# Input transform of a convolution, Fourier and MLP kernel: eight input pieces in four buffers instead of four pieces in two

## The chip, the cores and the metric

The kernel runs on one core of a Trainium2 chip. The time is device microseconds (us) of one execution; a kernel's time is the median of its runs. Before the change the median of three runs is 1305.61 us (1303.28, 1305.61 and 1310.38).

## The reference, cut to what matters

The input x has 8 batches of 4224 tokens with 192 features. Eight heads of 24 features each get a causal convolution over seven tokens, with softmaxed weights. On its result follow a Fourier transform over tokens and features, a layer norm and an MLP of 768 hidden units:

```python
    x_unf = x_pad[:, idx, :].reshape(B, S, K, H, group)
    out = np.einsum('hk,bskhg->bshg', w, x_unf)      # convolution
...
    X = np.fft.fft(x, axis=1)
    X = np.fft.fft(X, axis=2)
    mixed = np.real(X).astype(np.float32)
    u = x + mixed
    mu = np.mean(u, axis=-1, keepdims=True)
    var = np.mean((u - mu) ** 2, axis=-1, keepdims=True)
    un = (u - mu) / np.sqrt(var + 1e-06)
    ch = np.maximum(un @ w_ch1, 0.0) @ w_ch2
    return (u + ch).astype(np.float32)
```

## The kernel before

The work is done batch by batch, and each batch passes through stages:

- **Convolution** (`conv_unit`, matmul at L389). Six chunks a batch, each in three parts; an input tile `xt` is multiplied with a band matrix, copied out of the accumulators into `xa` (by ScalarE, L397) and stored from there to a scratch tensor `sc` in device memory. `squares` (L345) sums squares of the input, from which `scales` makes the batch's scale. Batch 7 does its last head in another way, on VectorE (`conv_segments`), and stores that with L423.
- **Loading the transform's input** (`load_x`, L458). The scratch is read back with another layout: 128 partitions by 33 blocks of 192 values. Before the change the 33 blocks are cut into four pieces of 9, 8, 8 and 8 (`PIECES`), each read by four transfers of 32 partitions. The pieces lie in tiles `xs`, for which there are two buffers. So piece 2 can only be loaded when the splits of piece 0 have been done.
- **Split** (`split_x`). ScalarE writes the high half of an input as float16 to `XH` (L474), VectorE the remainder to `XL` (L475). Each piece is split in two halves of 4 or 5 blocks. `XH` and `XL` exist once; they hold a whole batch.
- **Stage A** (`stage_a`, matmul at L492, then L500 on ScalarE and L501 on VectorE): sixteen units a batch, the first part of the Fourier transform over tokens. It needs all 33 blocks, so all splits. **Stage B** (`stage_b`, L518, L526, L527): eight units a batch.
- **Prep** (`prep`): the transform over features (L608), the addition to the convolution's rows `u` (L625; the rows were fetched from the scratch by L553 and, indirectly, by GpSimd at L557), the norm (L632, L633, and GpSimd at L643 to L665), and a transposing DMA `kt<-hl` (L675) issued by SyncE.
- **MLP** (`mlp_hidden`, matmul L704 into `ph`, ScalarE's `hh` at L708, VectorE's `hlo` at L709; `mlp_out`, matmuls L723, L726, L729 into `po`, VectorE L735), then the store of `u` by SyncE (L743). `ph` has two buffers, and one becomes free when `hlo` has read it.

The main loop has 72 steps: nine steps `it` = 0 to 8 for each of eight batches, the ninth (`it` = 8) a short one with a quarter of the tokens. In step n stand the hidden layer of step n and the output layer of step n-1; between their units are spread the other batches' earlier stages, by tables that tell at which step, counted relative to the first step of their own batch, a stage is done (`conv_at`, `load_at`, `split_at`, `a_at`, `b_at`; `load_1`, `split_1`, `a_1` for batch 1). So `load_at = {-10: [0], -9: [1, 2], -8: [3]}` puts the load of piece 0 ten steps ahead of its own batch. Batch 0 is worked through ahead of the loop, without anything to lie beside.

From this the program's order on each engine is made by a scheduler when the kernel is built; it may draw an instruction forward when its operands and buffers are there, or let it stand later. What it makes is a fixed list for each engine. An engine works its list in order, and so does SyncE (SP): a DMA that waits for a buffer holds up every DMA that stands behind it on SP.

## Time and profile before

| | |
|---|---|
| median of three runs | 1305.61 us |
| the profiled execution's own time | 1310.74 us |
| its span, from first to last instruction | 1308.4 us |
| TensorE (PE) busy | 1191.7 us, 91% |
| VectorE (DVE) busy | 828.9 us, 63% |
| GpSimd (POOL) busy | 794.4 us, 61% |
| ScalarE (ACT) busy | 585.2 us, 45% |
| mean granted TensorE clock | 0.963 |
| DMA | 130 GB/s mean, up to 277 GB/s in a fortieth of the span |

The rows of the profile name an engine, a line of the kernel, and the tiles as out<-in. "Idle before" is the engine's idle time ahead of an instruction, and the arrow names what ended it. Lines in the waits view read: who waited, for whom, us in total, times, longest. The windows view gives for a stretch of time its length, then the busy time of each engine with the number of instructions, the granted clock (1.00 is full, 0.50 half), the DMA engines' busy share and their rate. SPq and ACTq are DMA issues on those engines.

### The profile page before, as it was taken

The page shows a single profiled execution, that of the slowest core. Times are in us where ns is not written, and L with a number is a line of the kernel's source. Part 1 is how long each engine was busy: PE and PEld are TensorE (multiplying, and loading weights), DVE is VectorE, ACT ScalarE, POOL GpSimd, SP SyncE. Part 2 cuts the span into 40 slices and gives each one's busy share as a digit, 9 for nine tenths or more (in the row PEclk, how much of TensorE's full clock was granted, in tenths as well). Part 3 has the DMA queues.
Part 4 walks back from the last instruction along what each step waited for, and adds up shares of the span by engine and source line. Part 5 has one row for each costly group of instructions (what it writes and reads, how often), then busy time and mean ns, then how long its engine had stood idle before and what let it go on. Part 6 is the DMA issues. An engine that isn't in the chain of part 4 may idle for free.

```text
span 1308.4 us, 30213 instructions
## 1 busy us (share of the span) xinstructions
PE 1191.7 (91%) x12224; PEld 938.2 (72%) x12224; DVE 828.9 (63%) x1883; ACT 585.2 (45%) x962; POOL 794.4 (61%) x1116
## 2 busy tenths in 40 slices
PE   4168889997999989999899989999889998999998
PEld 4156768785877768787677858778677876778767
DVE  7746586467555776467755676556865678666543
ACT  4632375336543464435544355444644445333222
POOL 0236666577645785468664777547955589657850
PEclk9578999998999989999899999999899999999999
DMA  8924966357546465446644664563664444323231
GB/s 277 263 69 107 206 182 160 109 129 159 127 122 135 122 156 153 127 104 176 133 132 107 140 177 105 145 129 100 167 150 117 121 101 91 84 65 87 56 75 40
DMA packets 238363, 170.29 MB, mean 130 GB/s; under 512 B 119688, under 2 KB 222032, under 8 KB 238224
## 3 DMA queue, kind: packets, MB, share of 16 engines
q1 hardware_dynamic: 182096, 121.22, 38.5%
q10 hardware_dynamic: 49600, 33.77, 9.3%
q0 software_dynamic: 6528, 13.38, 3.9%
q8 instruction: 95, 1.56, 0.5%
q14 instruction: 44, 0.36, 0.1%
HBM read 83.82 MB, written 58.55 MB: 109 GB/s over the span
## 4 chain that ended last, share of the span: by engine, by line
PE 74%; DMA 9%; DVE 8%; ACT 3%; issue 2%; another core or an unknown queue 1%; ACTq 1%; POOL 1%; SPq 1%; DVEq 0%; POOLq 0%
PE ph L704 28%; PE po L723 8%; PE po L729 8%; PE po L726 8%; DMA xs<-sc 6%; PE pa L492 6%; PE pc L389 5%; PE pb L518 5%; PE pq L608 5%; DVE XL L475 3%; DVE u L625 2%; ACT XH L474 2%; DMA sc<-xa 1%; DVE hlo L709 1%
## 5 line engine op out<-in xcount | busy, mean ns | idle before, releaser
L704 PE MATMUL ph<-kt,W 128*128 128x512 f16 (+1 forms) x2160 | 504.9, 367 | 22.3 <-DVE hlo L709 17.1
L709 DVE SCALAR_TENSOR_TENSOR hlo<-ph,hh 128x512 f16<-128x512 f32 (+1 forms) x400 | 272.3, 681 | 295.6 <-ACT hh L708 274.1
L708 ACT ACTIVATE hh<-ph 128x512 f16<-128x512 f32 (+1 forms) x400 | 236.2, 592 | 453.0 <-PE ph L704 408.0
L723 PE MATMUL po<-W,hh 128*128 128x192 f16 x1584 | 387.8, 247 | 16.9 <-ACT hh L708 16.7
L729 PE MATMUL po<-W,hlo 128*128 128x192 f16 x1584 | 387.3, 247 | 1.5 <-DVE hlo L709 1.2
L726 PE MATMUL po<-W,hh 128*128 128x192 f16 x1584 | 387.4, 247 | 0.0
L704 PEld LDWEIGHTS <-W 128*128 128x128 f16 x2160 | 194.5, 99 | 169.9 <-issue 20.5
L652 POOL TENSOR_SCALAR un<-u,mv,y 128x192 f32<-128x192 f32 x264 | 279.0, 1063 | 7.9 <-POOL y L648 0.2
L557 POOL DMA_INDIRECT u<-sc,rows_sb x136 | 144.6, 1063 | 195.5 <-DMA xt<-in_xw_dram 56.4
L723 PEld LDWEIGHTS <-hh 128*128 128x128 f16 x1584 | 156.1, 99 | 40.2 <-ACT hh L708 18.5
L729 PEld LDWEIGHTS <-hlo 128*128 128x128 f16 x1584 | 155.7, 98 | 22.8 <-issue 1.8
L726 PEld LDWEIGHTS <-hh 128*128 128x128 f16 x1584 | 155.6, 98 | 16.6 <-issue 0.7
L389 PE MATMUL pc<-xt,band 128*120 128x144 f32 x756 | 116.2, 295 | 25.8 <-DMA band<-line_d 14.8
L492 PE MATMUL pa<-c_sb,XH 128*128 128x128 f16 x1024 | 105.0, 224 | 31.3 <-ACT XH L474 18.3
L389 PEld LDWEIGHTS pc<-xt,band 128*120 128x120 f32 x756 | 104.2, 188 | 35.2 <-issue 16.0
L475 DVE SCALAR_TENSOR_TENSOR XL<-xs,s_x,XH 128x768 f16<-128x768 f32 x64 | 102.8, 1620 | 41.2 <-ACT XH L474 41.1
L665 POOL TENSOR_TENSOR hl<-un,hl 128x512 f16<-128x512 f32 (+1 forms) x144 | 122.2, 870 | 2.8
L474 ACT ACTIVATE XH<-xs,s_x 128x768 f16<-128x768 f32 x64 | 105.4, 1689 | 26.6 <-DMA xs<-sc 26.6
L501 DVE SCALAR_TENSOR_TENSOR yl<-pa,yh 99x512 f16<-99x512 f32 x128 | 85.7, 684 | 46.0 <-ACT yh L500 35.8
L500 ACT ACTIVATE yh<-pa 99x512 f16<-99x512 f32 x128 | 75.5, 598 | 87.3 <-PE pa L492 63.6
L643 POOL TENSOR_SCALAR v<-mv 128x4 f32<-128x4 f32 (+1 forms) x72 | 20.7, 287 | 152.9 <-DVE mv L633 150.2
L492 PEld LDWEIGHTS <-XH 128*128 128x128 f16 x1024 | 83.2, 100 | 38.6 <-ACT XH L474 18.4
(120 smaller groups left out, 1496.2 us busy)
## 6 DMA issues: line engine op xcount, KB each, us to landing
out_dram<-u SPq DMA_DIRECT2D x64, 384.0 KB
xt<-in_xw_dram SPq DMA_DIRECT2D x42, 576.0 KB
sc<-xa ACTq DMA_DIRECT2D x42, 540.0 KB
xs<-sc SPq DMA_DIRECT2D x96, 192.0 KB
xs<-sc SPq DMA_DIRECT2D x32, 216.0 KB
u<-sc SPq DMA_DIRECT2D x72, 96.0 KB
sc<-xa ACTq DMA_DIRECT2D x7, 450.0 KB
xt<-in_xv_dram SPq DMA_DIRECT2D x6, 504.0 KB
```

Source lines behind the costliest of these rows:

```text
L389: nc.tensor.matmul(pc[:WR, h - h0], band[:, h, :WR], xt[:, :, h * GRP : (h + 1) * GRP], start=True, stop=True,)
L474: split = nc.scalar.activation(part(XH), src, AF.Copy, scale=bt.c)
L475: nc.vector.scalar_tensor_tensor(part(XL), src, bt.c, part(XH), op0=ALU.mult, op1=ALU.subtract)
L492: nc.tensor.matmul(pa[:, i], x[:, at], F[:, l], start=(n == 0), stop=(n == 2))
L557: nc.gpsimd.indirect_dma_start(to, None, bt.sc[:S], bass.IndirectOffsetOnAxis(ap=rows_sb[:, col : col + 1], axis=0),)
L652: nc.gpsimd.tensor_scalar(un[:, g], u[:, g], mv[:, g, 0:1], y[:, g : g + 1], op0=ALU.subtract, op1=ALU.mult,)
L704: nc.tensor.matmul(ph[:, n], W1[:, w, ht * 128 : (ht + 1) * 128], kt[:, k], start=(i == 0), stop=(i == len(order) - 1),)
L708: anchor[0] = nc.scalar.activation(hh, ph, AF.Relu).ins
L709: nc.vector.scalar_tensor_tensor(hlo, ph, 0.0, hh, op0=ALU.max, op1=ALU.subtract)
L723: nc.tensor.matmul(po[:, g % 2], hh[:, ht, tk], W2[:, ht, 0], start=(ht == 0), stop=False)
L726: nc.tensor.matmul(po[:, g % 2], hh[:, ht, tk], W2[:, ht, 1], start=False, stop=False)
L729: nc.tensor.matmul(po[:, g % 2], hlo[:, ht, tk], W2[:, ht, 0], start=False, stop=(ht == 5),)
```

## The change

The pieces become eight of 4 or 5 blocks, each split at once. There are four `xs` buffers of at most 5 blocks in place of two of 9. A piece is read by one transfer over all 128 partitions, or by two where its token numbers wrap around. The loads stand at steps -11 to -8, two pieces a step, and each is split one step later, at -10 to -7; stage A takes the two steps -6 and -5 in place of three. For batch 1 the loads are at steps -8 and -7, the splits at -7 and -6, stage A in one step. `conv_segments` stands two steps earlier relative to the scales. In batch 0 the last four pieces lie in halves of two tiles that are free at that time.

```diff
-PIECES = ((0, 9), (9, 17), (17, 25), (25, 33))
+PIECES = ((0, 4), (4, 9), (9, 13), (13, 17), (17, 21), (21, 25), (25, 29), (29, 33))
...
-        x = sb.tile([128, SH, DH], F32, tag="xs", name=f"xg_{bt.b}", bufs=2)
+        x = sb.tile([128, SH, DH], F32, tag="xs", name=f"xg_{bt.b}", bufs=4)
...
-        tag, bufs = (("yh", 1), ("yl", 1))[i - 2] if b == 0 and i > 1 else ("xs", 2)
-        xs = sb.tile([NA, 9, D], F32, tag=tag, name=f"xs_{b}_{i}", bufs=bufs)
-        for ch in range(NA // AC):
-
-            first = 33 * AC * ch + 128 * b0 - (S if b0 >= WRAP[ch] else 0)
+        if b == 0 and i in (4, 6):
+            bt.wide = sb.tile(
+                [NA, 9, D], F32, tag=("yh", "yl")[i // 2 - 2], name=f"xs_{b}_{i}", bufs=1
+            )
+            xs = bt.wide[:, :4]
+        elif b == 0 and i in (5, 7):
+            xs = bt.wide[:, 4:8]
+        else:
+            xs = sb.tile([NA, 5, D], F32, tag="xs", name=f"xs_{b}_{i}", bufs=4)
+        cut = next(c for c in range(5) if c == 4 or b0 >= WRAP[c])
+        for c0, c1, wrap in ((0, cut, 0), (cut, 4, S)):
+            if c0 == c1:
+                continue
             src = bass.AP(
                 bt.sc.tensor,
-                bt.sc.offset + first * D,
-                [[33 * D, AC], [128 * D, b1 - b0], [1, D]],
+                bt.sc.offset + (33 * AC * c0 + 128 * b0 - wrap) * D,
+                [[33 * D, AC * (c1 - c0)], [128 * D, b1 - b0], [1, D]],
             )
...
     def split_x(bt, i):
-        i, half = divmod(i, 2)
-        first = PIECES[i][0]
-        b0, b1 = ((first, first + 4), (first + 4, PIECES[i][1]))[half]
-        src = bt.xs[i][:, b0 - first : b1 - first].rearrange("p b (t j) -> p j (b t)", t=ND)
+        b0, b1 = PIECES[i]
+        src = bt.xs.pop(i)[:, : b1 - b0].rearrange("p b (t j) -> p j (b t)", t=ND)
...
-    load_at = {-10: [0], -9: [1, 2], -8: [3]}
-    split_at = {-9: [0, 1], -8: [2, 3, 4, 5], -7: [6, 7]}
-    a_at = {-7: range(0, 4), -6: range(4, 10), -5: range(10, 16)}
+    load_at = {-11: [0, 1], -10: [2, 3], -9: [4, 5], -8: [6, 7]}
+    split_at = {-10: [0, 1], -9: [2, 3], -8: [4, 5], -7: [6, 7]}
+    a_at = {-6: range(0, 8), -5: range(8, 16)}
...
-    load_1 = {-9: [0, 1], -8: [2, 3]}
-    split_1 = {-8: [0, 1], -7: [2, 3, 4, 5], -6: [6, 7]}
-    a_1 = {-6: range(0, 6), -5: range(6, 16)}
+    load_1 = {-8: [0, 1, 2, 3], -7: [4, 5, 6, 7]}
+    split_1 = {-7: [0, 1, 2, 3], -6: [4, 5, 6, 7]}
+    a_1 = {-5: range(16)}
...
+        if rel == max(conv) - 1 and bt.b >= NB0:
+            units.append(call(conv_segments, bt))
         if rel == max(conv) + (bt.b > 1):
-            if bt.b >= NB0:
-                units.append(call(conv_segments, bt))
             units.append(call(scales, bt))
```

What the scheduler makes of it is shown for batch 3, whose input is loaded and split while batch 1 ends and batch 2 begins. In a name the first number is the batch, the second the piece, step or chunk: `xs_3_2` is piece 2 of batch 3, `kt_2_3` the transposed input of step 3 of batch 2. The line numbers of the changed kernel are six higher for most of these (L466 for L458, L480 for L474, L481 for L475).

On SP, where the transposes for steps 2 and 3 of batch 2 are issued, there stood before:

```order
L675 DMA_TRANSPOSE kt_2_2_5842<-hl_2_2_5759 128x12x128
L332 DMA xt_4_1_5900<-in_xw_dram 128x1152
L458 DMA xs_3_2_5853<-sc_3_3791 32x8x192 x4
L458 DMA xs_3_3_5974<-sc_3_3791 32x8x192 x4
L743 DMA out_1_dram<-u_2_0_4765 128x768
L675 DMA_TRANSPOSE kt_2_3_6032<-hl_2_3_5968 128x12x128
L332 DMA xt_4_2_6155<-in_xw_dram 128x1152
```

At the same place there stands now:

```order
L466 DMA xs_3_6_5983<-sc_3_3787 32x4x192
L466 DMA xs_3_6_5983<-sc_3_3787 96x4x192
L466 DMA xs_3_7_6018<-sc_3_3787 32x4x192
L466 DMA xs_3_7_6018<-sc_3_3787 96x4x192
L681 DMA_TRANSPOSE kt_2_2_5853<-hl_2_2_5772 128x12x128
L332 DMA xt_4_1_5909<-in_xw_dram 128x1152
L749 DMA out_1_dram<-u_2_0_4769 128x768
L681 DMA_TRANSPOSE kt_2_3_6040<-hl_2_3_5977 128x12x128
L332 DMA xt_4_2_6161<-in_xw_dram 128x1152
```

Before, the second half of the input (pieces 2 and 3) is issued behind the transpose for step 2; now only the last quarter is left here, and it stands ahead of that transpose. Pieces 0 to 3 stand ahead of `kt_2_0`, and pieces 4 and 5 around `kt_2_1`.

On ScalarE (ACT), in steps 1 and 2 of batch 2, where before the split halves 2 to 7 stand:

```order
L708 ACTIVATE hh_2_1_5902<-ph_2_1_1_5979 128x512
L474 ACTIVATE XH_106<-xs_3_1_5837,s_x3_5471 128x64x12 x2
L708 ACTIVATE hh_2_1_5902<-ph_2_1_2_6037 128x512
L708 ACTIVATE hh_2_1_5902<-ph_2_1_3_6076 128x512
L345 ACTIVATE sq_4_0_6086,nrm_4_6085<-xt_4_0_5689 128x1152
L474 ACTIVATE XH_106<-xs_3_2_5853,s_x3_5471 128x64x12 x2
L708 ACTIVATE hh_2_1_5902<-ph_2_1_4_6124 128x512
L708 ACTIVATE hh_2_1_5902<-ph_2_1_5_6147 128x512
L708 ACTIVATE hh_2_2_6157<-ph_2_2_0_6159 128x512
L474 ACTIVATE XH_106<-xs_3_3_5974,s_x3_5471 128x64x12 x2
```

there stand now pieces 4, 5 and the first of the last two:

```order
L714 ACTIVATE hh_2_1_5911<-ph_2_1_1_5986 128x512
L480 ACTIVATE XH_106<-xs_3_4_5850,s_x3_5390 128x64x12
L714 ACTIVATE hh_2_1_5911<-ph_2_1_2_6045 128x512
L480 ACTIVATE XH_106<-xs_3_5_5864,s_x3_5390 128x64x12
L345 ACTIVATE sq_4_0_6084,nrm_4_6083<-xt_4_0_5702 128x1152
L714 ACTIVATE hh_2_1_5911<-ph_2_1_3_6092 128x512
L714 ACTIVATE hh_2_1_5911<-ph_2_1_4_6130 128x512
L714 ACTIVATE hh_2_1_5911<-ph_2_1_5_6153 128x512
L397 ACTIVATE xa_4_1_6271<-pc_4_1_0_6272 120x3x6x24
L714 ACTIVATE hh_2_2_6163<-ph_2_2_0_6165 128x512
L480 ACTIVATE XH_106<-xs_3_6_5983,s_x3_5390 128x64x12
```

Four of the eight splits have moved out of these two steps, to the short step and step 0 ahead of them; between the split of piece 0 and that of piece 4, which takes its buffer, lies a whole step.

On VectorE (DVE), from the end of the short step of batch 1 to step 0 of batch 2, there stood no split:

```order
L632 BN_STATS st_2_2_5642<-u_2_2_5282 128x6 x2
L735 SCALAR_TENSOR_TENSOR u_1_7_4191<-po_1_7_0_5502,fo_393,u_1_7_4191 128x384
L633 BN_AGGR mv_2_2_5643<-st_2_2_5642 128x2 x4
L735 SCALAR_TENSOR_TENSOR u_1_7_4191<-po_1_7_2_5623,fo_393,u_1_7_4191 128x384
L709 SCALAR_TENSOR_TENSOR hlo_2_0_5692<-ph_2_0_0_5693,hh_2_0_5691 128x512
```

and now two stand there, ahead of the first `hlo` of step 0:

```order
L481 SCALAR_TENSOR_TENSOR XL_107<-xs_3_0_5435,s_x3_5390,XH_106 128x64x12
L638 BN_STATS st_2_2_5656<-u_2_2_5286 128x6 x2
L741 SCALAR_TENSOR_TENSOR u_1_7_4150<-po_1_7_0_5510,fo_393,u_1_7_4150 128x384
L481 SCALAR_TENSOR_TENSOR XL_107<-xs_3_1_5483,s_x3_5390,XH_106 128x64x15
L639 BN_AGGR mv_2_2_5657<-st_2_2_5656 128x2 x2
L741 SCALAR_TENSOR_TENSOR u_1_7_4150<-po_1_7_2_5637,fo_393,u_1_7_4150 128x384
L715 SCALAR_TENSOR_TENSOR hlo_2_0_5705<-ph_2_0_0_5706,hh_2_0_5704 128x512
```

The splits of pieces 0 and 1 have moved into the short step, which had none.

## The prediction

> **What bounds the kernel now.** I began with the page's busy times and with who waited for whom on TensorE between 200 and 1200 us, the part in which batches follow each other evenly.

> ```profile
> PE 1191.7 (91%) x12224; PEld 938.2 (72%) x12224; DVE 828.9 (63%) x1883; ACT 585.2 (45%) x962; POOL 794.4 (61%) x1116
> PE po L723 <- ACT hh L708: 16.7, 6, 4.3
> PE ph L704 <- DVE hlo L709: 14.2, 7, 2.6
> ```

> TensorE is the bound, and it waits in few and long waits: six for `hh`, seven for `hlo`, about one of each a batch. The timelines of one such place, in step 1 of batch 2, show why: first SyncE, then VectorE, ScalarE and TensorE.

> ```profile
> 434.84 1.45 SPq L675 DMA_TRANSPOSE kt<-hl  x1
> 453.09 1.46 SPq L675 DMA_TRANSPOSE kt<-hl  x1
> 458.10 7.72 SPq L458 DMA_DIRECT2D xs<-sc  x8
> 468.15 1.58 SPq L675 DMA_TRANSPOSE kt<-hl  x1
> ...
> 452.95 1.69 DVE L475 SCALAR_TENSOR_TENSOR XL<-xs,s_x,XH 128x768 f16<-128x768 f32 x1
> 456.21 1.86 DVE L475 SCALAR_TENSOR_TENSOR XL<-xs,s_x,XH 128x960 f16<-128x960 f32 x1
> 473.75 0.67 DVE L709 SCALAR_TENSOR_TENSOR hlo<-ph,hh 128x512 f16<-128x512 f32 x1
> ...
> 464.55 0.19 ACT L345 ACTIVATION_READ_ACCUMULATOR sq<-xt 128x1 f32 x1
> 467.78 3.10 ACT L474 ACTIVATE XH<-xs,s_x 128x768 f16<-128x768 f32 x2 [3.04 <-DMA xs<-sc]
> 470.79 1.05 ACT L708 ACTIVATE hh<-ph 128x512 f16<-128x512 f32 x2
> ...
> 471.41 0.26 PE L723 MATMUL po<-W,hh 128*128 128x192 f16 x1 [3.33 <-ACT hh L708]
> 474.49 1.89 PE L704 MATMUL ph<-kt,W 128*128 128x512 f16 x4 [2.57 <-DVE hlo L709]
> ```

> The second split half of piece 0 ends on VectorE at 456.21 + 1.86 = 458.07. At 458.10 SyncE issues the eight transfers of pieces 2 and 3: they had waited for the buffer. ScalarE comes to the split of piece 2 at 464.74 and stands until 467.78, since the data are still on their way. Behind it in ScalarE's list stand two `hh`, done only after 470.79; TensorE is idle until 471.41, and once more until 474.49, for `hlo`, which VectorE does behind its own splits. The wait is a buffer's, and it repeats in every batch.

> The windows view prices it. I cut each place into the idle stretch and the slow stretch after it; columns are the length, busy PE, PEld, DVE, ACT, POOL with counts, then granted clock, DMA share and rate. The last row is batch 7's, which has no slow stretch.

> ```profile
> 312.27:319.69 7.42, 0.83 (x5) 0.44 (x5) 5.08 (x9) 4.06 (x4) 1.23 (x2) 0.70 1.23 225
> 319.69:325.44 5.75, 5.75 (x20) 2.91 (x21) 3.82 (x11) 3.40 (x3) 5.34 (x9) 0.50 0.10 30
> 468.09:474.49 6.40, 0.51 (x5) 0.29 (x5) 5.09 (x9) 3.75 (x4) 2.00 (x3) 0.82 1.08 250
> 474.49:479.04 4.55, 4.55 (x16) 2.28 (x17) 2.62 (x11) 2.20 (x3) 4.22 (x8) 0.50 0.09 23
> 621.68:627.54 5.86, 0.51 (x4) 0.28 (x4) 5.08 (x9) 3.21 (x4) 0.30 (x1) 0.85 1.28 200
> 627.54:632.64 5.10, 5.10 (x17) 2.55 (x18) 3.17 (x11) 2.75 (x3) 4.77 (x8) 0.50 0.27 97
> 775.27:781.50 6.23, 0.51 (x6) 0.29 (x5) 5.10 (x9) 3.56 (x4) 2.19 (x3) 0.83 1.05 263
> 781.50:786.24 4.74, 4.74 (x16) 2.39 (x17) 2.81 (x11) 2.39 (x3) 4.41 (x8) 0.50 0.07 21
> 928.79:934.73 5.94, 0.50 (x4) 0.28 (x5) 5.16 (x9) 3.22 (x4) 4.39 (x4) 0.86 0.99 234
> 934.73:939.84 5.11, 5.11 (x17) 2.54 (x18) 3.18 (x11) 2.76 (x3) 4.78 (x8) 0.50 0.44 136
> 1080.51:1086.80 6.29, 2.98 (x24) 2.10 (x25) 6.29 (x12) 4.41 (x5) 6.12 (x5) 1.00 0.70 181
> ```

> Idle, as length less PE busy: 6.59, 5.89, 5.35, 5.72, 5.44, and 3.31 in batch 7. In the slow stretches PE is busy throughout at clock 0.50, so half their length is lost: 2.88, 2.28, 2.55, 2.37, 2.56. A place costs 9.5, 8.2, 7.9, 8.1, 8.0 and 3.3 us; together 44.9 us.

> **The change part by part.** *Buffers and loads in the even part.* Four buffers let pieces 0 to 3, half the input, land before any split. A later piece needs the buffer of the piece four before, which is split a whole step earlier. Steps come out of ScalarE's list, six `hh` a step and two in the short one; here the short step of batch 1, then steps 0, 1 and 2 of batch 2:

> ```profile
> 430.70:437.90 7.20, 6.85 (x81) 6.26 (x81) 5.44 (x18) 1.32 (x4) 3.59 (x6) 1.00 0.36 69
> 437.90:454.70 16.80, 16.46 (x192) 12.52 (x190) 12.63 (x32) 9.68 (x15) 13.98 (x21) 1.00 0.42 117
> 454.70:476.90 22.20, 16.30 (x133) 11.49 (x131) 17.21 (x35) 12.05 (x17) 16.88 (x21) 0.89 0.94 229
> 476.90:494.20 17.30, 17.30 (x160) 13.26 (x159) 10.57 (x14) 11.24 (x17) 15.45 (x19) 0.94 0.35 76
> ```

> So a load has about 17 us until its split. From the first issue at 458.10 to the split at 467.78 it took 9.7 us for piece 2, with all eight transfers in flight. What was late should come some 7 us early. I take the 44.9 us as gone. Nothing else is near: outside these places PE is full in these rows, and the totals of VectorE, ScalarE and GpSimd leave room. The same matmuls, splits and stage A units are done as before.

> *Splits in the short step.* This is the new cost. VectorE is busy 5.44 of 7.20 us in the short step and 12.63 of 16.80 in step 0. Two splits (1.69 + 1.86 = 3.55 us) come into the short step, ahead of the first `hlo` of step 0, while step 0 keeps its two: 21.6 of 24.0 us. Queued behind them are `hlo` (which frees `ph` for TensorE) and the two halves' `u` sums. Step 1 loses four and falls from 17.21 to about 14. The cost lies between 0 (VectorE's 4.2 us of idle in step 0 takes it up) and 3.55 a batch; a gain is excluded because the relief of step 1 is already in the 44.9. I take 1.0, nearer to 0 as the sum still fits, for six batches: +6.0 us, at most +21.3.

> *SyncE's queue.* The loads of pieces 4 to 7 wait for splits, and with them the transposes behind them. `kt` for step 1 was issued at 434.84 and is needed when that step begins, 454.70: 19.9 us ahead. `kt` for step 2, at 453.09, is needed at 476.90 less the 8 us gained, about 469: 16 us ahead. The eight issues took 7.72 us; four now stand ahead of the second, and a wait for the split of piece 3 at the end of step 0. That uses some 8 of 16 us. I count nothing; the rival below is what happens if the cover goes. Fewer issues (fourteen for sixteen a batch) are worth nothing, since SyncE is not waited for.

> *Stage A in two steps.*

> ```profile
> L501 DVE SCALAR_TENSOR_TENSOR yl<-pa,yh 99x512 f16<-99x512 f32 x128 | 85.7, 684 | 46.0 <-ACT yh L500 35.8
> L500 ACT ACTIVATE yh<-pa 99x512 f16<-99x512 f32 x128 | 75.5, 598 | 87.3 <-PE pa L492 63.6
> ```

> Eight units a step instead of six add two evictions each on VectorE and ScalarE, 1.4 and 1.2 us on engines that are busy 10.57 and 11.24 of 17.30 us in step 2, which has four units: hidden, 0. Starting one step later still ends in the same step ahead of stage B.

> *Batch 1.* Its stretch holds waits for `xt`, `kt` and the same splits:

> ```profile
> 149.78:188.39 38.61, 29.13 (x218) 21.26 (x217) 24.37 (x46) 22.38 (x27) 24.31 (x30) 0.91 0.93 232
> ```

> 9.5 us idle and (1 - 0.91) x 38.61 = 3.5 at half clock, 13 us. The tables put its loads, its first splits and its first stage A units one step later, and on SyncE batch 2's `xt` now stand ahead of the loads: both take waits away. But all sixteen stage A units fall into one step, and DMA runs at 0.93 there. Bounds 0 and 13; I take half, 6.5.

> *Batch 0*, ahead of the loop, has nothing beside it.

> ```profile
> 34.86 12.39 SPq L458 DMA_DIRECT2D xs<-sc  x16
> 66.00:82.00 16.00, 4.78 (x43) 3.08 (x42) 1.40 (x3) 3.27 (x8) 9.63 (x11) 0.71 0.48 133
> ```

> Piece 0 was complete with the ninth issue of sixteen in the list, now with the fifth: at best 4/16 x 12.39 = 3.1 us earlier. Against it, the 11.2 idle us of 66 to 82 follow nothing that the splits release, and could grow as well. I take 0, between -3 and +3.

> *`conv_segments`* stands earlier, but its store keeps ScalarE as long, with a wait behind it:

> ```profile
> 956.94 7.19 ACTq L423 DMA_DIRECT2D sc<-sg  x1
> 964.18 0.60 ACT L500 ACTIVATE yh<-pa 99x512 f16<-99x512 f32 x1 [7.76 <-issue]
> PE pa L492 <- DVE yl L501: 3.6, 1, 3.6
> ```

> The 3.6 us on TensorE stay: 0, give or take 3.

> The sum: 1310.74 (the profiled execution) - 44.9 - 6.5 + 6.0 = 1265.3. That execution lies 5.13 us above the median of the runs, 1305.61; less that, **1260** us, 3.5% faster.

> **The rivals.** *All of it:* no cost in the short step, batch 1 whole, batch 0 by 3: 1310.74 - 44.9 - 13 - 3 - 5.13 = 1245. For it, the lists put every load a step ahead; against it, something is usually late next, and VectorE at 90% is near.

> *Half:* VectorE's list makes `hlo` late, in the short step and after, so that half of each wait comes back. 44.9/2 + 6.5/2 = 25.7 is gained and 6.0 paid: 1310.74 - 19.7 - 5.13 = 1286. For it, the second part of each wait was on `hlo` (2.57 at 474.49). Against it, that `hlo` stood behind two splits that were themselves late from the load. [...]

> *Slower:* SyncE. In place of ScalarE's wait for the load comes TensorE's wait for `kt`, held behind loads that wait for splits. If a transpose comes up at the end of its cover and has a train like that of 458.10 ahead of it (7.72 us), is then issued for 1.58 us, and lands 2.0 us after (as piece 2 did after the last of its train: 467.78 less 458.10 + 7.72), TensorE waits 11.3 us and loses 2.5 more at half clock: 13.8 against 8.2 removed, +5.6 in six batches, and nothing gained in batch 1: 1305.6 + 34 = 1339. It comes out slower than before once TensorE waits over 5.7 us (with the 2.5 at half clock, the 8.2 removed), which takes transposes 14 us later than I have them. Against it, that 8 of 16 us of cover are left. [...]

> *No change:* ScalarE's wait moves to another load, and the time with it: 1300 to 1311.

> **How the numbers follow.** Forecast 0.60, all of it 0.13, half 0.15, no change 0.05, slower 0.07. The range from 1244 (all of it) to 1290 (half, at 1286, with 4 us more of the short step's cost) leaves out no change, slower and the tails, under 0.2. A measurement of this kernel can tell about 0.5% from no change (6.5 us; the three runs spread 7.1). Faster 0.88, same 0.05, slower 0.07.

> **What would show it.** Right: no wait of ScalarE's XH for `xs<-sc` after 300 us; PE full and clock 1.00 through steps 0 to 2; step 1 near 17 us instead of 22.20; loads of pieces 0 to 3 issued before the short step. Wrong: TensorE waits for `kt`; `hlo` waits of over 1 us a batch in the short step and step 0; a half clock after 300 us; steps as long as before.

## The result, and the profile after

The changed kernel takes 1273.99 us (median of four runs, 1272.1 to 1276.18), the kernel before, in four runs beside them, 1307.99: a ratio of 0.974, 95% interval 0.970 to 0.978. Forecast were 1260 us and a range of 1244 to 1290. The direction and the range held; 14 us of the forecast gain did not come. The profiled execution of the changed kernel took 1275.37 us, with a span of 1273.6 and a mean granted clock of 0.976.

The busy times on the page of the changed kernel:

```profile
PE 1179.2 (93%) x12224; PEld 934.7 (73%) x12224; DVE 833.3 (65%) x1883; ACT 589.6 (46%) x962; POOL 789.9 (62%) x1116
```

TensorE is busy 12.5 us less (1191.7 before), with the same matmuls. Its waits from 200 to 1200 us:

```profile
PE pc L389 <- DMA xt<-in_xw_dram: 10.1, 4, 3.4
PE ph L710 <- DVE hlo L715: 2.9, 5, 1.1
PE po L729 <- ACT hh L714: 2.6, 2, 2.0
PE po L735 <- DVE hlo L715: 2.0, 1, 2.0
PE pc L389 <- DMA xt<-in_xv_dram: 1.8, 1, 1.8
```

The waits for `hh` and `hlo` that carried the forecast, 16.7 and 14.2 us, have shrunk to 2.6 and 4.9. A wait that the kernel before did not have in this part took their place: the convolution's matmuls `pc` wait five times for their input `xt`, 11.9 us in all. ScalarE's split XH no longer waits for `xs` after 300 us.

The windows view of the short step of batch 1 and steps 0, 1 and 2 of batch 2 (length, then busy PE, PEld, DVE, ACT, POOL with counts, granted clock, DMA share and rate), to set beside the same four rows of before:

```profile
418.30:426.40 8.10, 8.10 (x107) 7.42 (x105) 5.80 (x14) 4.90 (x6) 4.65 (x6) 1.00 0.14 39
426.40:443.00 16.60, 16.60 (x195) 13.03 (x193) 16.27 (x43) 9.54 (x15) 11.39 (x17) 1.00 0.72 181
443.00:459.90 16.90, 15.30 (x134) 11.47 (x132) 13.08 (x30) 9.55 (x15) 15.80 (x23) 1.00 0.80 199
459.90:474.20 14.30, 14.30 (x132) 10.70 (x131) 9.38 (x12) 9.72 (x15) 13.14 (x14) 1.00 0.62 162
```

Step 1 is 16.90 us in place of 22.20 and runs at full clock. Its remaining idle time, 16.90 - 15.30 = 1.6 us, is one wait for `xt`. Step 0 has VectorE busy 16.27 of 16.60 us and is no longer than before; the short step is 0.9 us longer, with 26 more matmuls in it and TensorE busy throughout. SyncE's timeline in the changed kernel ahead of that wait:

```profile
431.70 0.41 SPq L332 DMA_DIRECT2D xt<-in_xw_dram  x1
...
441.84 3.92 SPq L466 DMA_DIRECT2D xs<-sc  x4
447.11 4.46 SPq L681 DMA_TRANSPOSE kt<-hl  x1
451.62 1.36 SPq L332 DMA_DIRECT2D xt<-in_xw_dram  x1
```

TensorE's timeline, the matmul that waited:

```profile
457.00 0.38 PE L389 MATMUL pc<-xt,band 128*120 128x144 f32 x1 [1.60 <-DMA xt<-in_xw_dram]
```

The row at 451.62 is `xt_4_1`, and the convolution that needs it comes up on TensorE at 455.40. Ahead of it in SyncE's list stand the four loads of pieces 6 and 7, and `kt_2_2`, whose issue ended at 451.57, 0.05 us before. The row of the loads merges four issues, which the trace has as 0.30 to 0.43 us each: two went out at 441.84 and 442.22, after VectorE's split of piece 2 had ended at 441.81, and two at 444.98 and 445.33, after that of piece 3 had ended at 444.95. So 2.3 of the 3.92 us are a wait for a buffer. But at 445.76 the loads are through, and `kt_2_2` is issued only at 447.11, because GpSimd's `hl`, which it transposes, is done at 447.09. A row of VectorE's timeline and two of GpSimd's show why that is late:

```profile
426.25 1.88 DVE L481 SCALAR_TENSOR_TENSOR XL<-xs,s_x,XH 128x960 f16<-128x960 f32 x1
429.55 0.24 POOL L649 TENSOR_SCALAR v<-mv 128x4 f32<-128x4 f32 x1 [6.30 <-DVE mv L639]
445.30 1.79 POOL L671 TENSOR_TENSOR hl<-un,hl 128x512 f16<-128x512 f32 x2
```

In VectorE's order `mv_2_2` stands behind the two splits that moved into the short step. GpSimd waits for it and begins the norm 3.2 us after the first `hh` of batch 2; before, it began 1.3 us ahead of that `hh` (436.59 against 437.9). `hl` is done 20.7 us after the first `hh`, before at 15.2. The issue of `kt_2_2` then took 4.46 us, where it had taken 1.46. In batch 1 it is the same; in batches 3 to 5 the loads end 1.1 to 3.3 us after `hl`, so that there they hold the transpose up as well.

Where the 34.8 us of span went, by three stretches: up to the first `hh` of batch 1, batches 1 to 6, and batch 7. First the kernel before, then the changed one:

```profile
0.00:282.10 282.10, 207.89 (x2088) 169.88 (x2089) 178.96 (x415) 127.94 (x209) 130.90 (x188) 0.90 0.64 168
282.10:1191.50 909.40, 870.14 (x9067) 683.90 (x9065) 588.60 (x1326) 425.09 (x698) 603.88 (x834) 0.98 0.52 127
1191.50:1308.40 116.90, 113.65 (x1075) 84.45 (x1072) 61.38 (x143) 32.17 (x56) 59.64 (x94) 1.00 0.25 64
```

```profile
0.00:276.80 276.80, 205.75 (x2089) 168.54 (x2090) 179.22 (x410) 130.94 (x211) 132.61 (x186) 0.90 0.65 169
276.80:1156.00 879.20, 859.69 (x9067) 681.69 (x9065) 592.72 (x1333) 426.50 (x696) 597.70 (x836) 1.00 0.53 132
1156.00:1273.60 117.60, 113.78 (x1075) 84.47 (x1072) 61.33 (x143) 32.13 (x56) 59.62 (x94) 1.00 0.25 63
```

Batches 1 to 6 gave 909.4 - 879.2 = 30.2 us: TensorE's idle time fell from 39.3 to 19.5 us, and its busy time, with the same matmuls, by 10.4, of which 9.7 is less half clock. The start with batch 0 gave 5.3; batch 7 took 0.7 back.

### The profile page after: what moved, and what is told of

Same layout as the page of the kernel before. It is cut to its first block, busy times and chain, and to the rows that moved or that the text cites. A ratio compares the mean times of both kernels' runs of the same rounds, so it can differ in the third digit from the quotient of the medians.

```text
span 1273.6 us, 30194 instructions
## 1 busy us (share of the span) xinstructions
PE 1179.2 (93%) x12224; PEld 934.7 (73%) x12224; DVE 833.3 (65%) x1883; ACT 589.6 (46%) x962; POOL 789.9 (62%) x1116
## 4 chain that ended last, share of the span: by engine, by line
PE 75%; DVE 9%; DMA 5%; POOL 4%; issue 4%; ACT 2%; ACTq 1%; SPq 0%; DVEq 0%; POOLq 0%
PE ph L710 28%; PE po L729 9%; PE po L735 8%; PE po L732 8%; PE pa L498 7%; PE pc L389 6%; PE pq L614 5%; PE pb L524 4%; DMA xt<-in_xw_dram 3%; DVE XL L481 2%; DVE u L631 2%; DMA xs<-sc 1%; DVE hlo L715 1%; DVE st L638 1%; POOL un L658 1%
## 5 line engine op out<-in xcount | busy, mean ns | idle before, releaser
L710 PE MATMUL ph<-kt,W 128*128 128x512 f16 (+1 forms) x2160 | 494.7, 362 | 3.8 <-DVE hlo L715 3.6
L563 POOL DMA_INDIRECT u<-sc,rows_sb x136 | 145.4, 1069 | 189.6 <-DMA out_dram<-u 66.6
L389 PE MATMUL pc<-xt,band 128*120 128x144 f32 x756 | 118.4, 297 | 36.5 <-DMA band<-line_d 14.8
L671 POOL TENSOR_TENSOR hl<-un,hl 128x512 f16<-128x512 f32 (+1 forms) x144 | 124.9, 888 | 2.8
L498 PE MATMUL pa<-c_sb,XH 128*128 128x128 f16 x1024 | 105.2, 225 | 20.5 <-ACT XH L480 13.5
L481 DVE SCALAR_TENSOR_TENSOR XL<-xs,s_x,XH 128x768 f16<-128x768 f32 x64 | 106.6, 1673 | 18.5 <-ACT XH L480 18.3
L631 DVE SCALAR_TENSOR_TENSOR u<-pq,g,u 128x128 f32<-128x128 f32 (+1 forms) x328 | 102.9, 380 | 11.1 <-PE pq L614 8.7
L480 ACT ACTIVATE XH<-xs,s_x 128x768 f16<-128x768 f32 x64 | 106.1, 1681 | 8.1 <-DMA xs<-sc 8.1
```

The source lines that it names most:

```text
L389: nc.tensor.matmul(pc[:WR, h - h0], band[:, h, :WR], xt[:, :, h * GRP : (h + 1) * GRP], start=True, stop=True,)
L481: nc.vector.scalar_tensor_tensor(part(XL), src, bt.c, part(XH), op0=ALU.mult, op1=ALU.subtract)
L498: nc.tensor.matmul(pa[:, i], x[:, at], F[:, l], start=(n == 0), stop=(n == 2))
L563: nc.gpsimd.indirect_dma_start(to, None, bt.sc[:S], bass.IndirectOffsetOnAxis(ap=rows_sb[:, col : col + 1], axis=0),)
L631: nc.vector.scalar_tensor_tensor(to, src, bt.g, to, op0=ALU.mult, op1=ALU.add)
L710: nc.tensor.matmul(ph[:, n], W1[:, w, ht * 128 : (ht + 1) * 128], kt[:, k], start=(i == 0), stop=(i == len(order) - 1),)
```

## The experiments

Theory A on the missing gain: SyncE's list, in order, put `xt` behind loads and a transpose that are late. Rival theories are stated with each run. The kernels ran in three groups, each on one chip beside runs of the kernel before, whose medians were 1308.29, 1285.79 and 1309.62 us. In the second group all kernels had a shorter start (batch 1 began at 261 to 265 us, in the others at 276 to 282), so between groups I compare ratios and, free of the start, the time from batch 1's first `hh` to the end of the profiled span. That time is of one execution, and depends on the group a little too: one kernel, the one with both of the first two edits, took 977.5 us in the second group and 981.9 in the third. The two rows without a group are the runs of the result.

| kernel | group | median us | ratio to before (95%) | from batch 1 to the end, us |
|---|---|---|---|---|
| before | | 1307.99 | 1 | 1026.3 |
| changed | | 1273.99 | 0.974 (0.970 to 0.978) | 996.8 |
| changed, once more | 3 | 1273.94 | 0.975 (0.972 to 0.979) | 989.4 |
| `xt` early | 1 | 1261.05 | 0.963 (0.961 to 0.966) | 982.3 |
| stage A in three steps | 1 | 1265.73 | 0.969 (0.966 to 0.972) | 984.4 |
| both of these | 2 | 1241.11 | 0.965 (0.962 to 0.968) | 977.5 |
| both, once more | 3 | 1262.50 | 0.964 (0.961 to 0.967) | 981.9 |
| before, with `xt` early | 3 | 1304.86 | 0.997 (0.995 to 0.999) | 1020.0 |
| old steps, eight pieces, four buffers | 1 | 1300.36 | 0.994 (0.992 to 0.996) | 1022.2 |
| two buffers | 1 | 1281.24 | 0.979 (0.976 to 0.982) | 1005.1 |
| two buffers, `xt` early | 2 | 1259.85 | 0.980 (0.977 to 0.983) | 991.2 |
| four transfers a piece | 2 | 1251.30 | 0.972 (0.969 to 0.975) | 991.2 |
| `xt` early, segments late | 2 | 1241.48 | 0.965 (0.962 to 0.968) | 976.4 |
| both, split doubled | 3 | 1273.47 | 0.974 (0.971 to 0.977) | 991.1 |

**`xt` early.** Both first chunks of a batch's convolution input are issued in one step, so that the second stands ahead of the loads.

```diff
-                if ch == rel - min(conv) + 2 or bt.b == 2:
+                if rel == min(conv) - 2 or bt.b == 2:
```

> One edit to the changed kernel: the convolution's input chunk 1 of a batch is loaded together with chunk 0, one step earlier, ahead of the loads of pieces 6 and 7 and of the transpose on SyncE. Theory A (the new wait is one of SyncE's order: xt stands behind loads that wait for splits, while its matmuls were drawn forward): the five waits of TensorE for xt after 300 us (11.9 us and 3.4 us at half clock in the changed kernel) go, and the median falls from 1274 to about 1260, ratio to before 0.963. Theory B (the DMA engines have no room there, so a transfer issued earlier only delays others): 8 us or more of waits for xt, xs or kt stay, and the time is 1270 to 1276.

It takes 1261.05 us, 13 less than the changed kernel. TensorE's waits from 200 to 1200 us:

```profile
PE ph L710 <- DVE hlo L715: 4.5, 6, 1.5
PE ph L710 <- DMA kt<-hl: 2.2, 1, 2.2
PE po L729 <- ACT hh L714: 1.4, 2, 0.8
PE pa L498 <- DVE XL L481: 0.5, 1, 0.5
```

SyncE's timeline at the same place of the program:

```profile
431.42 1.06 SPq L332 DMA_DIRECT2D xt<-in_xw_dram  x2
...
442.94 2.32 SPq L466 DMA_DIRECT2D xs<-sc  x4
448.70 1.47 SPq L681 DMA_TRANSPOSE kt<-hl  x1
```

The wait for `xt` is gone, with no half clock from 200 us to just ahead of the end, and the loads still arrive in time. So the missing gain was an order on SyncE, not a lack of transfer time. The line puts `xt` ahead of the loads and of `kt` alike, so it does not tell what each of them cost. One wait for `kt`, of 2.2 us, shows that its cover is not unlimited either.

**Stage A in three steps.** The other end of the same wait: the table of before, for all batches but 0 and 1.

```diff
-    a_at = {-6: range(0, 8), -5: range(8, 16)}
+    a_at = {-7: range(0, 4), -6: range(4, 10), -5: range(10, 16)}
```

> One edit to the changed kernel: stage A in the three steps it had before (4, 6 and 6 units); for batch 1 it stays in one step. In TensorE's list the convolution of chunk 1 then stands behind the hidden units of step 2 again, not ahead of them. Theory A: the waits for xt after 300 us go, because the matmuls come later though the load does not come earlier; about 1261, ratio 0.964. The prediction's own reading (stage A in two steps costs nothing, all hidden): as the changed kernel, 1274. Theory B (no room on the DMA engines): 1270 to 1276, with the waits elsewhere.

1265.73 us. SyncE's list is as in the changed kernel; in batch 2 `xt_4_1` is issued as late as there:

```profile
439.28 5.82 SPq L466 DMA_DIRECT2D xs<-sc  x4
445.22 5.10 SPq L681 DMA_TRANSPOSE kt<-hl  x1
450.36 0.57 SPq L332 DMA_DIRECT2D xt<-in_xw_dram  x1
```

Yet TensorE does not wait for it, since stage A units stand ahead of the convolution again: it begins at 464.09, 13.2 us after this issue had ended, and in the changed kernel it was asked for 2.4 us after it. The wait needed both: the load later, and its consumer earlier. In batch 5 this kernel has a wait of its own, 4.0 us for `hlo` with 6.83 us of half clock behind it.

**Both together.**

> The changed kernel with both edits that had each ended TensorE's wait for the convolution's input xt: both chunks loaded two steps earlier (1261.05 us alone) and stage A back in three steps (1265.73 alone). Theory A, both removed one and the same wait of some 15 us (11.9 idle and 3.4 at half clock): together they give no more than the better of them, 1257 to 1266. Theory B, stage A in two steps has a price of its own besides (two more evictions a step on VectorE and ScalarE): the gains add, 1273.99 - 12.9 - 8.3 = 1253, and under 1256.

> The kernel with xt early and stage A in three steps once more, the base of the doubled split below. Both theories expect its ratio of before, 0.9648 (0.9617 to 0.9679), batches 1 to 4 of 144.5 us each and no wait of TensorE in them.

0.965 and 0.964, no better than `xt` early alone (0.963): the two edits removed the same wait, and stage A in two steps has no other price that can be measured. In the first of these, batches 1 to 4 took 144.5 us each with no wait of TensorE over 0.3 us. In the second, one batch took 146.6 and one 145.4, with waits of 0.5 to 1.2 us.

**Before, with `xt` early.** The same one line in the kernel before.

> The kernel before the change, with one edit alone: both xt chunks of each batch loaded two steps earlier. Theory A, the wait for xt was made by the change (the last loads moved ahead of xt on SyncE, and the convolution drawn forward), so before it nothing waits for xt in the even part: 0.995 to 1.003 of the kernel before. Theory B, early xt is a gain of its own that has nothing to do with the change: 0.985 to 0.99, some 13 us as in the changed kernel.

0.997 (0.995 to 0.999): 4 to 5 us, not 13. TensorE waits for `xt` in the even part neither with the line nor without it; the old waits stay, shifted:

```profile
PE po L723 <- ACT hh L708: 11.2, 6, 2.7
PE po L723 <- DVE u L735: 6.0, 6, 1.5
```

So the change itself made the wait for `xt`.

**Old steps, with eight pieces and four buffers.** The tables of loads, splits and stage A of before, batch 1's too, each old piece now being two:

```diff
-    load_at = {-11: [0, 1], -10: [2, 3], -9: [4, 5], -8: [6, 7]}
-    split_at = {-10: [0, 1], -9: [2, 3], -8: [4, 5], -7: [6, 7]}
+    load_at = {-10: [0, 1], -9: [2, 3, 4, 5], -8: [6, 7]}
+    split_at = {-9: [0, 1], -8: [2, 3, 4, 5], -7: [6, 7]}
...
```

> Eight pieces, four buffers and the one or two transfers of the changed kernel, but loads, splits and stage A at the steps of the kernel before, for batch 1 too. If the buffers carry the gain (half the input lands ahead of any split): ScalarE's waits for xs shrink from about 5 us a batch to under 2, no half clock, 1265 to 1280. If the steps carry it: the waits stay, 1295 to 1308.

The expectation that the buffers carry the gain fell: 1300.36 us. TensorE's largest wait:

```profile
PE po L729 <- ACT hh L714: 17.3, 6, 4.2
```

ScalarE's wait for `xs`, after 300 us:

```profile
ACT XH L480 <- DMA xs<-sc: 15.2, 10, 2.0
```

With four buffers a load that stands one step later is still under way when ScalarE comes to its split, and the two `hh` behind it are late as before.

**Two buffers.** The other half alone: all steps of the changed kernel, `bufs=2` for every `xs`.

```diff
-            xs = sb.tile([NA, 5, D], F32, tag="xs", name=f"xs_{b}_{i}", bufs=4)
+            xs = sb.tile([NA, 5, D], F32, tag="xs", name=f"xs_{b}_{i}", bufs=2)
...
```

> The changed kernel with two xs buffers in place of four (also for the tiles of the convolution that share them); pieces, transfers and steps as changed. If the buffers carry the gain: ScalarE waits for xs in each batch again, as a piece is issued only when the one two before it is split, 1285 to 1300. If the steps carry it: as the changed kernel, 1270 to 1278.

1281.24 us, so the steps give more than the buffers. But the wait of before is here as well, under another name, in the waits of TensorE:

```profile
PE po L729 <- DVE u L741: 18.4, 6, 4.2
```

ScalarE's timeline in step 1 of batch 2:

```profile
452.83 1.60 ACT L480 ACTIVATE XH<-xs,s_x 128x768 f16<-128x768 f32 x1 [4.39 <-DMA xs<-sc]
```

VectorE stands behind the same late piece, with the `u` sum that frees `po` behind its XL.

**Two buffers, with `xt` early.**

> The changed kernel with xt early and two xs buffers in place of four. With four buffers and xt late it took 1273.99, with two and xt late 1281.24, so that the buffers seemed worth 7 us. Theory A, the wait for xt had hidden most of what the buffers are worth: with two buffers TensorE waits for u and ScalarE for xs, 3 to 4 us in five batches, xt or no xt, so the early xt gives next to nothing here, 1277 to 1284, and the buffers are worth 16 to 23 us once xt is there. Theory B, the two waits are separate places and add: 1261.05 + 7.3 = 1268.

By the ratio, 0.980 against 0.979, the early `xt` gave nothing here, as theory A had it. The time from batch 1 on says otherwise: 1005.1 without it, 991.2 with it, 14 us, as much as with four buffers (996.8 to 982.3). The traces have a gain too, but not in a wait for `xt`: with two buffers TensorE does not wait for `xt` in this part in either kernel. Its wait for `u` falls from 18.4 to 5.8 us and half clock from 17.1 us to none (in batch 2 the granted clock is 0.99 and 1.00), while the waits for `hlo` grow from 4.2 to 9.1. SyncE's list differs in more than `xt`, five loads behind `kt_2_2` in place of four, so what the early `xt` itself gave is open. Batch 2 in the windows view, two buffers with `xt` late, two with `xt` early, and four with `xt` early:

```profile
425.70:577.60 151.90, 146.65 (x1535) 116.43 (x1533) 98.11 (x222) 74.42 (x122) 96.64 (x139) 0.99 0.56 137
```

```profile
412.50:560.60 148.10, 145.17 (x1533) 115.49 (x1531) 98.10 (x222) 74.21 (x121) 97.19 (x139) 1.00 0.57 141
```

```profile
407.70:552.30 144.60, 144.60 (x1534) 115.53 (x1531) 98.50 (x222) 74.03 (x121) 98.92 (x139) 1.00 0.56 144
```

The ratios are from two groups, and the starts differ in the opposite sense: among the kernels of its group the one with two buffers was the earliest to begin batch 1 in the first (275.9) and the latest in the second (265.1). What the second pair of buffers is worth: with `xt` late 7.3 us in time (1281.24 less 1273.99, beside runs of before that agree to 0.3 us) and 8.3 from batch 1 on; with `xt` early 18.4 (1259.85 less 1241.48, in one group) and 14.8. So the waits seem to overlap: where TensorE waits for `u`, `xt` has landed when it is asked for. That is not settled, since two profiled executions of the changed kernel differ by as much, 996.8 and 989.4 us from batch 1 on; against the second, the buffers are worth 15.7 us with `xt` late, no less than with it early.

**Four transfers a piece,** of 32 partitions each, as in the kernel before.

```diff
-        for c0, c1, wrap in ((0, cut, 0), (cut, 4, S)):
+        for c0, c1, wrap in ((c, c + 1, 0 if c < cut else S) for c in range(4)):
```

> The changed kernel with each piece read by four transfers of 32 partitions, as before, in place of one or two (32 issues a batch in place of 14). Theory A, what counts is how long SyncE's list is ahead of xt and kt: the four issues of the last two pieces took 3.92 us, eight take some 7.7, so xt comes about 4 us later in five batches, and the half clock follows each: 1273.99 + 5 x 4 to 5 x 7 = 1294 to 1309. Theory B, the larger transfers are worth nothing by themselves, since the same bytes move and SyncE's time is hidden: 1271 to 1277.

0.972 (0.969 to 0.975) against 0.975 (0.972 to 0.979) for the changed kernel once more: no difference. `xt` is waited for five times here as well, 11.1 us, not 4 us more each. SyncE's issues ahead of it tell why:

```profile
427.11 7.79 SPq L466 DMA_DIRECT2D xs<-sc  x7
435.01 2.08 SPq L681 DMA_TRANSPOSE kt<-hl  x1
437.13 0.96 SPq L332 DMA_DIRECT2D xt<-in_xw_dram  x1
```

From the first load to the end of `kt`'s issue it is 10.0 us with seven issues, and was 9.7 with four (441.84 to 451.57). Both rows of loads hold a wait for the split of a piece, 2.2 us here and 2.3 there, which theory A took for issue time. The issues alone are 5.4 us for seven and 1.5 for four. What the larger transfers saved on them came back on the transpose, 4.46 us in place of 2.08, and in its wait of 1.35 us for `hl`, which has no counterpart here.

**The changed kernel once more,** beside the others of the third group.

> The changed kernel once more, beside the others of this call on one chip. Both theories expect its ratio of before, 0.9741 (0.9697 to 0.9784); even batches 2 and 3 of 146 to 148 us, with TensorE's wait for xt in five batches. If the kernel with four transfers (0.9719) is faster than it, this ratio is above 0.977.

0.975, as before. It waits for `xt` five times, 8.1 us in place of 11.9, with one stretch of half clock behind them in place of two.

**`xt` early, `conv_segments` late.**

```diff
-        if rel == max(conv) - 1 and bt.b >= NB0:
-            units.append(call(conv_segments, bt))
         if rel == max(conv) + (bt.b > 1):
+            if bt.b >= NB0:
+                units.append(call(conv_segments, bt))
             units.append(call(scales, bt))
```

> The changed kernel with xt early and conv_segments back at its place of before, two steps later relative to the scales. Theory A (the step 'conv_segments: 0, give or take 3' holds): in the early-xt kernel TensorE waits 1.6 us around that place (0.37, 0.46 and 0.82 at 902 to 908 us), before it was 3.65 us at 961.91, so it comes back some 2 us slower, 1261 to 1265. Theory B, the earlier place collides with the loads and steps 1 and 2 of that batch, which are 15.2 and 18.5 us long against 13.5 and 15.0 in the batch with no conv_segments: up to 5 us faster without it there, 1256 to 1259.

0.965, beside 0.963 for `xt` early: the earlier place of `conv_segments` neither costs nor gives what can be measured, and theory B falls.

**The split doubled in the short step.** VectorE's XL of pieces 0 and 1 is done twice in batches 2 to 7, on the kernel with both edits; the values stay the same.

```diff
-        nc.vector.scalar_tensor_tensor(
-            part(XL), src, bt.c, part(XH), op0=ALU.mult, op1=ALU.subtract
-        )
+        for _ in range(2 if bt.b > 1 and i < 2 else 1):
+            nc.vector.scalar_tensor_tensor(
+                part(XL), src, bt.c, part(XH), op0=ALU.mult, op1=ALU.subtract
+            )
```

> The kernel with xt early and stage A in three steps, with VectorE's XL operations of pieces 0 and 1 done twice in each of batches 2 to 7 (same result): 3.4 us more on VectorE in the short step, ahead of the first hlo of step 0. VectorE is busy 7.60 of the last 8.7 us and 15.79 of step 0's 16.7, so 2.0 us are free until step 1. Theory A (slack, as the prediction's term on the short step had it): what exceeds the slack is paid, 1.4 us in six batches, +8 us, and step 0 near 18. Theory B (VectorE's list is in order and hlo stands behind it): all of it is paid, 3.4 x 6 = +20 us. Theory C (step 1, busy 11.50 of 13.70, takes it up as well): 0 to +3 us.

1273.47 us, 11 more than its base of 1262.50 in the same group. The short step of batch 1 and step 0 of batch 2, first the base, then this kernel:

```profile
417.50:425.50 8.00, 8.00 (x108) 7.41 (x106) 6.03 (x14) 4.90 (x6) 4.61 (x6) 1.00 0.16 47
425.50:442.20 16.70, 16.70 (x196) 13.12 (x194) 15.71 (x46) 9.58 (x15) 11.77 (x18) 1.00 0.84 220
```

```profile
414.90:423.00 8.10, 8.10 (x110) 7.51 (x107) 6.11 (x14) 4.97 (x6) 4.72 (x6) 1.00 0.42 96
423.00:442.00 19.00, 16.96 (x197) 13.27 (x194) 18.22 (x44) 9.46 (x15) 11.12 (x18) 1.00 0.61 169
```

Of the 3.4 us added, 19.00 - 16.96 = 2.04 show up as idle time of TensorE in one wait for `hlo` in step 0, and so in five batches (1.97 to 2.24; 1.53 in the sixth). Theory A's mechanism holds, with a price of about 2 us in place of 1.4; theories B and C fall. VectorE had not 2.0 us to spare there, but about 1.4.

## Why the prediction was right, and where it was short

**The waits for `hh` and `hlo`** (44.9 us taken as gone): right. Of 30.9 us of these waits between 200 and 1200 us 7.5 are left, 5.6 of them at the place of `conv_segments`. From 300 us to just ahead of the end, half clock is two stretches of 3.41 us in place of one of 10.24 and four of 6.83, and ScalarE's wait for `xs` is gone.

**"The wait is a buffer's":** half right. A second pair of buffers without the earlier steps gives 0.994; the steps without the buffers 0.979; both 0.974. The load's lead carried more than the buffer.

**SyncE's queue, "I count nothing":** this step failed. It weighed the cover of `kt` alone, though the order that it had before it shows `xt_4_1` in the same list, behind four loads and `kt_2_2`. The delay of some 8 us that it gave `kt_2_2` did come: against the start of step 1 its issue ends 8.7 us later than before (451.57 less 443.00 against 454.55 less 454.70), but 5.7 of them are `hl` and 3.0 the longer issue. The cover of `kt` held; that of `xt_4_1` behind it did not. The 7.72 us that the step counts for eight issues hold a wait as well, since the loads of piece 3 went out only from 463.34 on, when the last split of piece 1 had ended (463.31). The waits for `xt` cost 11.9 us in the profiled execution; behind two of them, of 2.98 and 3.39 us, the clock was half for 3.41 us each, and half of that was lost: 3.4. Together 15.3 us. Moving `xt` alone gave 13 us back. The rival "slower" had the mechanism in part, a transfer held on SyncE behind late ones, with the wrong transfer and far too high a price.

**Stage A in two steps, "hidden, 0":** this step failed too, though not by the evictions that it priced. With stage A out of step 2, `pc_4_1` came ahead of `ph_2_2_0` on TensorE, and the convolution asked for its input before it was there. Three steps gave back 8 us, and nothing more once `xt` was early.

**Splits in the short step,** 1.0 us in six batches: not paid where it was looked for. Step 0 stayed at 16.6 us with VectorE busy 16.27. The doubled split shows that the cover was real and nearly used up. But the term names only `hlo` and the `u` sums behind the splits and leaves out `mv_2_2`, and through it `hl`, `kt_2_2` and `xt_4_1` came later. In batches 1 to 5 the `hl` of step 2 is done 14.9 to 15.2 us after the first `hh` in the kernel before, 19.6 to 20.8 in the changed one, 15.4 to 15.7 with the old steps and four buffers, 20.2 to 20.9 with the new steps and two buffers. So the steps made it late, not the buffers; how much of the waits for `xt` is owed to it no run separates. "Step 1 loses four" is a miscount too, and so are the four splits said to leave steps 1 and 2: by the traces these two steps had seven splits and have five, step 1 five and now three. Its VectorE time, 13.08 us, came out near the 14 all the same.

**Batch 1 and batch 0** (6.5 and 0 us): together 5.3 us, by the first stretch of the windows. Batch 1's place still has a wait, in ScalarE's timeline of the changed kernel:

```profile
169.28 1.59 ACT L480 ACTIVATE XH<-xs,s_x 128x768 f16<-128x768 f32 x1 [6.79 <-DMA xs<-sc]
```

and in SyncE's:

```profile
156.29 6.43 SPq L681 DMA_TRANSPOSE kt<-hl  x1
162.77 3.64 SPq L466 DMA_DIRECT2D xs<-sc  x4
```

The loads went out 0.05 us after the issue of the transpose had ended, so here a transpose seems to have held the loads up, not the other way round. No run bears on it.

**`conv_segments`,** 0, give or take 3: the idle time at its place went from 3.65 us to 5.6 (1.96, 1.10, 0.56 and 2.01 between 906 and 925), and its old place is as good.

The account for batches 1 to 6: forecast 44.9 - 6.0 = 38.9, measured 30.2. The waits for `xt` took 15.3 and the place of `conv_segments` 2.0, while the 6.0 of the short step were saved: 38.9 - 15.3 - 2.0 + 6.0 = 27.6. Of the 2.6 us left over, 1.3 are idle time of TensorE outside all these places (3.3 us before, 2.0 now) and 1.2 its busy time (10.4 us less, of which the slow stretches as they were priced make 12.6 - 3.4 = 9.2). What made these two is open.

Of the signs named for being right, ScalarE's waits for `xs` are gone, step 1 is 16.90 us long, and the loads of pieces 0 to 3 are issued ahead of the short step. But step 1 is not full, and half clock comes twice after 300 us, both through `xt`, for which no sign was named. That the time still lies in the range is in part luck: the upper end was set by late `hlo` in the short step and after, of which the changed kernel shows next to nothing; the 14 us went mostly to a term counted as nothing.

## What to carry to other kernels

When a queue is filled earlier, go through every transfer that now stands behind it, not only the one that is known to be close, and ask of each what it waits for itself, who needs it, and whether that consumer has moved as well. A lead of one step and the buffer that allows it are two things; price them apart. A wait that is removed shows the next one, so run the changed kernel with that next wait taken away: one line here turned 0.974 into 0.963, faster than both kernels.

## What the runs showed of the hardware

```profile
305.81:309.22 3.41, 0.43 (x4) 0.35 (x4) 2.54 (x12) 0.60 (x1) 2.61 (x4) 1.00 0.54 202
309.22:312.63 3.41, 3.41 (x18) 2.61 (x17) 0.00 (x0) 0.53 (x1) 2.04 (x2) 0.50 0.08 21
749.55:752.96 3.41, 0.14 (x2) 0.00 (x0) 2.60 (x12) 0.60 (x1) 1.91 (x3) 1.00 1.04 298
752.96:756.37 3.41, 3.30 (x16) 3.01 (x17) 0.00 (x0) 0.53 (x1) 1.59 (x2) 0.50 0.13 52
```

```profile
147.48:150.89 3.41, 1.64 (x24) 1.14 (x21) 2.76 (x11) 1.09 (x3) 3.41 (x4) 1.00 0.97 205
150.89:154.30 3.41, 1.81 (x14) 1.70 (x15) 0.82 (x4) 1.86 (x4) 0.45 (x1) 1.00 0.84 314
154.30:157.71 3.41, 3.41 (x37) 2.77 (x36) 2.76 (x10) 2.13 (x5) 2.20 (x4) 1.00 0.41 102
```

The wait of 2.98 us at 305.89, inside one window, is followed by half clock. With `xt` early 1.77 and 1.60 us idle, in two windows one after the other, are not, and neither is the longer wait of 3.65 us in the kernel before (961.90 to 965.55), of which 1.82 us lie on each side of a border at 963.73. So of these waits not the longest cost clock, but the one of 2.98 us, which fell into one window. The grid's first border lies 1.17 us behind the start of the span in the trace of the kernel before and 2.02 us in that of the changed one.

**A transpose's issue is not of one length.** In the kernel before the median of 72 is 1.48 us, the longest 6.77. `kt_2_2`'s issue took 1.47 us where SyncE had been free for 3.4 us (448.70, `xt` early), 4.46 where it had been free for 1.35 us behind four loads, and 4.69 and 5.73 directly behind them in batches 3 and 4. With the small transfers the loads took longer, 7.79 us against 3.92, and the transpose less, 2.08 against 4.46. In the kernel before one took 4.05 us (141.77) after SyncE had been free for 6.2. What sets the length no run shows.
